# Joining every other pair of weight chunks on VectorE alone, two-byte stores for the rest, and idle matrix products around the first normalization

## The chip, the cores and the metric

The kernel runs on one core of one Trainium2 chip. The metric is the device time of one execution in microseconds, the median of the runs. The names used below: PE is TensorE (matrix products), PEld its weight loads, DVE is VectorE, ACT is ScalarE, POOL is GpSimd and SP the engine that issues most transfers.

## The reference, cut to what matters

Three layers follow each other on 8 batches of 576 tokens and 512 channels: an attention without a score matrix, a Fourier mixing with a normalization and a two-layer network, and a gated network at the end. The weights `w_ch1` and `w_ch2` come in float64 (`np.random.randn(...) * (1/np.sqrt(...))` stays 64 bits wide), which matters for the change.

```
kv  = einsum(softmax_over_tokens(k), v);  a = einsum(softmax_over_channels(q), kv)
u   = a + real(fft(fft(a, axis=1), axis=2))
un  = (u - mean(u)) / sqrt(var(u) + 1e-6)
x   = u + max(un @ w_ch1, 0) @ w_ch2
out = sigmoid(xr @ w_r) * ((max(xk @ w_k, 0) ** 2) @ w_v)      # xk, xr mix x with the token before
```

## The kernel before

The tokens of all batches, 4608, are cut into nine blocks of 512. The main loop takes block after block: for each of 16 column chunks `f` of `w_ch1`, `mm1(f)` makes `un @ w_ch1` (L1093), and two chunks later `mm2` multiplies the result by `w_ch2` (L1116). The last layer follows the same way (L1154, L1207, L1219). Once this loop runs, PE has always something to do, and the work of the next batches (attention, transform, norm) is done beside it.

Before the loop can run, four things must be ready, and they are made beside each other in a stretch that I call the front:

- `attention(0)` (L331 to L431) makes the first batch's `u` from q, k and v.
- `transform(0)` (L464 to L552) does the Fourier mixing as products with constant matrices: `eo`, `eh` and `el` are sums and their split into a rounded and a remaining part, `yh` and `yl` the result of the first products (L509), `pc` and `sd` those of the second (L529), and L545 to L552 add them to `u`.
- `norm(0)`, in two halves of 256 tokens: L616 makes the mean over channels as a product with a matrix of ones, L618 subtracts it into `d`, L620 and L621 square into `sq`, L632 makes the variance, again as a product with ones, L640 to L646 turn it into a reciprocal root `rs`, L658 scales `d`, and L671 and L672 split the result into `unh` and `unl`.
- `front_z` makes 32-bit floats from the 64-bit words of the two weight matrices, in 16 pairs of chunks (`pairs`, 128 x 1024 words each, numbered 0 to 15 here). A pair takes a low shift on DVE (L168), a store on ACT (L169), which writes the top three bits of the low word as one byte into the high word, a high join on DVE (L171), and a sum of squares on ACT (L231). After all pairs of a matrix a scale is known (`scales`, L240 to L250), and `split` (L257 on ACT, L258 on DVE) makes two 16-bit parts of each chunk. The first `mm1` needs the first four chunks split.

A scheduler fixes the order of the instructions of each engine when the program is built; on the chip each engine works through its own list in order and waits where an operand is not ready. So an edit in the front changes the order of all engines.

`warm` makes products whose result nobody reads, with the matrix of ones as the left operand; it writes into one of the two banks `h`. Before the change it stands at two places of the first batch's transform.

Of the kernel before, what the change touches and what calls it, by code (L numbers as in the profile page):

```python
# [10 lines left out]
F16 = mybir.dt.float16  # L11
BF16 = mybir.dt.bfloat16
U32 = mybir.dt.uint32
U8 = mybir.dt.uint8
AF = mybir.ActivationFunctionType
ALU = mybir.AluOpType
AX = mybir.AxisListType
# [11 lines left out]
POOL_K = ()  # L29
BEHIND_X = {(1, 1): 6}  # L30
RATE = 0.4
AHEAD_W = 6
FIRST = 1.0
HOLD = {(2, 0): "c"}
# [14 lines left out]
def net(ctx, tc, q, k, v, w1, w2, mu_k, mu_r, w_k, w_v, w_r, ce_d, se_d, cs_d, ss_d, alt_d, id_d, out):  # L49
    nc = tc.nc  # L50
# [27 lines left out]
    mm = nc.tensor.matmul  # L78
# [82 lines left out]
        nc.sync.dma_start(out=raw.rearrange("p n w -> p (n w)"), in_=src.bitcast(U32)[128 * t:128 * t + 128, 512 * c:512 * c + 512])  # L161
        return raw

    def assemble(raw, x, part=None):

        hi, lo = raw[..., 1], raw[..., 0]
        if part != 1:
            nc.vector.tensor_scalar(out=x, in0=hi, scalar1=3, scalar2=0x3FFFFFFF, op0=ALU.logical_shift_left, op1=ALU.bitwise_and)  # L168
            nc.scalar.activation(out=raw.bitcast(U8)[..., 4], in_=lo, func=AF.Copy, scale=0.9975 * 2.0 ** -29, bias=-0.49)  # L169
        if part != 0:  # L170
            nc.vector.scalar_tensor_tensor(out=x, in0=hi, scalar=0xC0000007, in1=x, op0=ALU.bitwise_and, op1=ALU.bitwise_or)  # L171

    def decode(raw, x):

# [4 lines left out]
    raws = {}  # L179
# [33 lines left out]
    def words_at(w, c):  # L213
        a, b = place[w, c] + 1, place[w, c + 1] + 1
        return wr[:, a:b + 1:b - a]

    def low_parts(k):

        if k < len(pairs):
            assemble(raws[k], words_at(*pairs[k]), 0)  # L220

    def high_parts(k):
        if 0 <= k < len(pairs):
            assemble(raws.pop(k), words_at(*pairs[k]), 1)
            if k + 4 >= AHEAD_W:
                load_pair(k + 4)

# [207 lines left out]
        done_att[0] = b  # L435
        yield 0

    def warm(x, src):

        pt = bank("h", 2)  # L440
        for _ in range(x):
            mm(out=pt[:, 0:128], lhsT=ones, rhs=src, start=True, stop=True)


    done_att = [-1]
# [2 lines left out]
    def transform(b):  # L448
# [11 lines left out]
        if b in (0, 1, 2):  # L460

            for t in range(4):
                for e, op in ((0, ALU.add), (1, ALU.subtract)):
                    tt(out=eo[:, e, t, 1:289], in0=u[:, t, 1:289], in1=u[:, t, S - 1:HALF - 1:-1], op=op)  # L464
                if t == 0 and b == 0:
                    warm(8, eo[:, 0, 0, 1:129])
                if t == 2:
                    nc.scalar.activation(out=x6[0:1, 0:289], in_=eo[0:1, 0, 2, 0:289], func=AF.Copy)
                    tt(out=x6[32:33, 0:289], in0=eo[0:1, 0, 2, 0:289], in1=x6[0:1, 0:289].bitcast(F32), op=ALU.subtract)
                yield 0  # L470
            nc.scalar.activation(out=eo[0:1, :, 2, 0:289], in_=eo[0:1, :, 3, 0:289], func=AF.Copy)
            nc.vector.memset(eo[0:1, 0, 3, 0:289], 0.0)
            for e, op in ((0, ALU.add), (1, ALU.subtract)):
                for g in range(2):
                    tt(out=eo[:, e, g, 0:289], in0=eo[:, e, g, 0:289], in1=eo[:, e, 3 - g, 0:289], op=op)
                    ma = nc.scalar.activation(out=eh[:, e, g, 0:289], in_=eo[:, e, g, 0:289], func=AF.Copy)
                    if b == 0:
                        warm(1, eo[:, e, g, 1:129])
                for g in range(2):
                    mv = tt(out=el[:, e, g, 0:289], in0=eo[:, e, g, 0:289], in1=eh[:, e, g, 0:289].bitcast(F32), op=ALU.subtract)  # L480
            if b < 2:
                mark((2, "a")[b], mv, ma)
            yield 0
        else:
            tt(out=eo[:, 0, :, 1:289], in0=u[:, :, 1:289], in1=back, op=ALU.add)
            yield 0
            tt(out=eo[:, 1, :, 1:289], in0=u[:, :, 1:289], in1=back, op=ALU.subtract)
            nc.scalar.activation(out=x6[0:1, 0:289], in_=eo[0:1, 0, 2, 0:289], func=AF.Copy)
            tt(out=x6[32:33, 0:289], in0=eo[0:1, 0, 2, 0:289], in1=x6[0:1, 0:289].bitcast(F32), op=ALU.subtract)
            nc.scalar.activation(out=eo[0:1, :, 2, 0:289], in_=eo[0:1, :, 3, 0:289], func=AF.Copy)  # L490
            nc.gpsimd.memset(eo[0:1, 0, 3, 0:289], 0.0)
            yield 0
            for e, op in ((0, ALU.add), (1, ALU.subtract)):
                tt(out=eo[:, e, 0:2, 0:289], in0=eo[:, e, 0:2, 0:289], in1=eo[:, e, 3:1:-1, 0:289], op=op)
            for e in range(2):
                nc.scalar.activation(out=eh[:, e, :, 0:289], in_=eo[:, e, 0:2, 0:289], func=AF.Copy)
                tt(out=el[:, e, :, 0:289], in0=eo[:, e, 0:2, 0:289], in1=eh[:, e, :, 0:289].bitcast(F32), op=ALU.subtract)
            yield 0
# [37 lines left out]
        for g in range(2):  # L536
# [2 lines left out]
            nc.scalar.activation(out=pc, in_=pp, func=AF.Copy)  # L539
            yield 1  # L540
            qq = stage2(slice(NK + 128 * g, NK + 128 * g + 128), ssh, ssl)
            tt(out=sd[:, g, 1, :], in0=pc, in1=qq, op=ALU.subtract)
            tt(out=sd[:, g, 0, :], in0=pc, in1=qq, op=ALU.add)
            yield 1
        tt(out=u[:, 0:2, 0:289], in0=u[:, 0:2, 0:289], in1=sd[:, :, 1, 0:289], op=ALU.add)  # L545
        tt(out=u[:, 0:2, S - 1:288:-1], in0=u[:, 0:2, S - 1:288:-1], in1=sd[:, :, 0, 1:288], op=ALU.add)
        pp = stage2(slice(0, 128), csh, csl)
        nc.scalar.activation(out=sd[0:1, 0], in_=sd[0:1, 1], func=AF.Copy)
        ma = nc.scalar.activation(out=sd[0:1, 1], in_=pp[0:1, None, :].to_broadcast([1, 2, NS]), func=AF.Copy)
# [49 lines left out]
    def norm_part(i, sq, d, rs, c0, n):  # L599
# [16 lines left out]
                    mm(out=pt[:, o - c0:o - c0 + m], lhsT=ones, rhs=U[b][:, t, s:s + m], start=(t == 0), stop=(t == 3))  # L616
        for b, s, m, o in segs:
            mv = tt(out=d[:, :, o:o + m], in0=U[b][:, :, s:s + m], in1=pt[:, None, o - c0:o - c0 + m].to_broadcast([128, 4, m]), op=ALU.subtract)  # L618
        yield 1
        nc.scalar.activation(out=sq[:, 0:2, cs], in_=d[:, 0:2, cs], func=AF.Square)  # L620
        ma = nc.scalar.activation(out=sq[:, 2:4, cs], in_=d[:, 2:4, cs], func=AF.Square)  # L621
        yield 0
        if not onpe:
# [14 lines left out]
        w = sq[:, 1, cs]  # L638
        if i in SUMS_F32:
            nc.scalar.activation(out=r, in_=pt[:, 0:n], func=AF.Ln, bias=wsc[:, 7:8])  # L640
            nc.scalar.activation(out=r, in_=r, func=AF.Exp, scale=-0.5)
            yield 1
            tt(out=v, in0=r, in1=r, op=ALU.mult)
            nc.vector.scalar_tensor_tensor(out=v, in0=pt[:, 0:n], scalar=1e-6, in1=v, op0=ALU.add, op1=ALU.mult)
            nc.vector.tensor_scalar(out=v, in0=v, scalar1=-0.5, scalar2=1.5, op0=ALU.mult, op1=ALU.add)
            tt(out=r, in0=r, in1=v, op=ALU.mult)  # L646
        else:
            nc.vector.tensor_scalar(out=v, in0=pt[:, 0:n], scalar1=1e-6, scalar2=None, op0=ALU.add)
            nc.scalar.activation(out=r, in_=v, func=AF.Ln)
# [6 lines left out]
        yield 0  # L656
        for x in range(2):
            (nc.gpsimd.tensor_tensor if i in POOL_N else tt)(out=d[:, 2 * x:2 * x + 2, cs], in0=d[:, 2 * x:2 * x + 2, cs], in1=r[:, None, :].to_broadcast([128, 2, n]), op=ALU.mult)  # L658
            yield 0
        if i == 0:  # L660
            halves_part(0, c0, n)
# [724 lines left out]
```

## Time and profile before

| what | us |
|---|---|
| median of 3 runs | 1475.55 (1475.35 to 1476.8) |
| the profiled execution, its own time | 1476.24 |
| span of that execution in the trace | 1474.5 |
| PE busy in the span | 1407.6 (95%) |
| DVE busy | 989.5 (67%) |
| ACT busy | 705.6 (48%) |

The span is the part of the execution that the trace covers; the profiled execution is 1.7 us longer than its span and 0.7 us above the median. The rate of TensorE's clock is given as the share of full speed that was granted: 1.00 is 2.4 GHz, 0.50 is 1.2 GHz. A matrix product of 32-bit floats shows as two MATMUL records in the trace and as one in the lists of instructions.

### The profile page before, as it was taken

The page shows a single profiled execution, that of the slowest core. Times are in us where ns is not written, and L with a number is a line of the kernel's source. Part 1 is how long each engine was busy: PE and PEld are TensorE (multiplying, and loading weights), DVE is VectorE, ACT ScalarE, POOL GpSimd, SP SyncE. Part 2 cuts the span into 40 slices and gives each one's busy share as a digit, 9 for nine tenths or more (in the row PEclk, how much of TensorE's full clock was granted, in tenths as well). Part 3 has the DMA queues.
Part 4 walks back from the last instruction along what each step waited for, and adds up shares of the span by engine and source line. Part 5 has one row for each costly group of instructions (what it writes and reads, how often), then busy time and mean ns, then how long its engine had stood idle before and what let it go on. Part 6 is the DMA issues. An engine that isn't in the chain of part 4 may idle for free.

```text
span 1474.5 us, 20917 instructions
## 1 busy us (share of the span) xinstructions
PE 1407.6 (95%) x8453; PEld 879.7 (60%) x8453; DVE 989.5 (67%) x1807; ACT 705.6 (48%) x1241; POOL 26.5 (2%) x41
## 2 busy tenths in 40 slices
PE   4559999998999999999999999999999999999998
PEld 3447888996555556556455444445666666666665
DVE  6778676587584765764532476774999788876643
ACT  6895643453342443432321246563766555564421
POOL 0101000000000000000000000000000000000000
PEclk8579999999999999999999999999999999999999
DMA  9731012121110111010010023301011011100001
GB/s 349 251 136 51 1 52 80 51 85 45 51 51 29 51 51 63 17 51 30 0 58 7 32 80 117 118 22 58 29 58 51 8 58 58 50 9 29 30 15 43
DMA packets 38301, 89.47 MB, mean 61 GB/s; under 512 B 5147, under 2 KB 11580, under 8 KB 38204
## 3 DMA queue, kind: packets, MB, share of 16 engines
q1 hardware_dynamic: 37052, 85.30, 16.6%
q0 software_dynamic: 1152, 2.83, 0.6%
q8 instruction: 66, 1.08, 0.3%
q14 instruction: 31, 0.25, 0.1%
HBM read 69.25 MB, written 18.87 MB: 60 GB/s over the span
## 4 chain that ended last, share of the span: by engine, by line
PE 88%; DVE 5%; ACT 4%; issue 1%; DMA 1%; ACTq 0%; DVEq 0%
PE h L1093 24%; PE acc L1116 24%; PE acc L1219 13%; PE h L1154 11%; PE side L1207 6%; PE side L509 2%; PE side L529 2%; PE side L430 2%; PE side L375 1%; ACT u L169 1%; PE side L410 1%; DVE wr L258 1%; DVE wr L171 1%; ACT words L169 1%; DMA kt<-in_k_dram 1%
## 5 line engine op out<-in xcount | busy, mean ns | idle before, releaser
L1093 PE MATMUL h<-unh,wr 128*128 128x512 f16 (+1 forms) x1408 | 381.8, 342 | 3.8 <-ACT unh L671 2.0
L1116 PE MATMUL acc<-hh,wr 128*128 128x512 f16 (+1 forms) x1408 | 370.4, 341 | 0.0
L1093 PEld LDWEIGHTS <-wr 128*128 128x128 f16 x2112 | 203.0, 98 | 169.1 <-issue 7.5
L1116 PEld LDWEIGHTS <-wr 128*128 128x128 f16 x2112 | 201.7, 98 | 160.8 <-issue 3.7
L1093 PE MATMUL h<-unl,wr 128*128 128x512 f16 (+1 forms) x704 | 240.6, 342 | 0.7 <-DVE unl L672 0.7
L1116 PE MATMUL acc<-hl,wr 128*128 128x512 f16 (+1 forms) x704 | 220.0, 341 | 0.0
L1219 PE MATMUL acc<-ring,last 128*128 128x512 f16 x864 | 201.2, 379 | 0.2 <-DVE last L1250 0.2
L1099 DVE SCALAR_TENSOR_TENSOR hl<-h,hh 128x512 f16<-128x512 f32 x144 | 99.0, 687 | 145.8 <-ACT hh L1098 145.2
L1098 ACT ACTIVATE hh<-h 128x512 f16<-128x512 f32 x144 | 85.8, 596 | 180.5 <-PE h L1093 179.8
L1219 PEld LDWEIGHTS <-last 128*128 128x128 f16 x864 | 84.0, 98 | 86.5 <-DVE last L1250 0.7
L1154 PEld LDWEIGHTS <-wkh 128*128 128x128 f16 x1008 | 98.5, 98 | 34.1
L1248 ACT ACTIVATE last<-last,pw 128x512 f32<-128x512 f32 x72 | 51.6, 717 | 106.9 <-DVE last L1247 106.3
L1207 PE MATMUL side<-ring,x 128*128 128x512 f16 x432 | 101.1, 379 | 0.0
L1154 PE MATMUL h<-x,wkh 128*128 128x256 f16 x560 | 95.7, 273 | 0.0
L1169 DVE TENSOR_TENSOR last<-h,last 128x512 f32<-128x512 f32 x90 | 61.8, 687 | 49.9 <-PE h L1154 49.8
L1154 PE MATMUL h<-x,wkl 128*128 128x256 f16 x280 | 76.3, 273 | 0.0
L1154 PE MATMUL h<-last,wkh 128*128 128x256 f16 x448 | 76.1, 273 | 0.0
L1207 PEld LDWEIGHTS <-x 128*128 128x128 f16 x432 | 42.3, 98 | 42.5
L1250 DVE TENSOR_TENSOR last<-last 128x512 f16<-128x512 f32 x72 | 49.5, 687 | 22.1 <-ACT last L1249 21.7
L1154 PE MATMUL h<-last,wkl 128*128 128x256 f16 x224 | 61.1, 273 | 0.0
L883 ACT ACTIVATE aa<-y,ms 128x512 f32<-128x512 f32 x72 | 48.0, 712 | 17.5 <-DVE x L891 12.2
L887 DVE SCALAR_TENSOR_TENSOR aa<-y,ms,aa 128x512 f32<-128x512 f32 x72 | 52.4, 747 | 1.2
(350 smaller groups left out, 2074.2 us busy)
## 6 DMA issues: line engine op xcount, KB each, us to landing
vt<-in_v_dram SPq DMA_DIRECT2D x16, 650.0 KB, 5.0
kt<-in_k_dram SPq DMA_DIRECT2D x16, 576.0 KB, 3.9
qt<-in_q_dram SPq DMA_DIRECT2D x16, 576.0 KB, 3.9
out_dram<-oo SPq DMA_DIRECT2D x36, 256.0 KB, 2.0
y<-yT SPq DMA_DIRECT2D x8, 1026.0 KB, 5.3
u<-in_w_dram SPq DMA_DIRECT2D x16, 512.0 KB, 4.5
words<-in_w_dram SPq DMA_DIRECT2D x10, 512.0 KB, 9.8
raw<-in_w_k_dram SPq DMA_DIRECT2D x16, 256.0 KB, 3.7
```

Source lines behind the costliest of these rows:

```text
L883: nc.scalar.activation(out=a, in_=y[:, t, 0:n], func=AF.Copy, scale=mu[:, w, 1, t:t + 1])
L887: nc.vector.scalar_tensor_tensor(out=a, in0=y[:, t, 1:n + 1], scalar=mu[:, w, 0, t:t + 1], in1=a, op0=ALU.mult, op1=ALU.add)
L1093: mm(out=pt[:, o:o + m], lhsT=a, rhs=c[:, t, o:o + m], start=(t == z == 0), stop=(t == 3 and z == 2))
L1098: ma = nc.scalar.activation(out=hh[:, 0:n], in_=pt[:, 0:n], func=AF.Relu)
L1099: mv = nc.vector.scalar_tensor_tensor(out=hl[:, 0:n], in0=pt[:, 0:n], scalar=0.0, in1=hh[:, 0:n], op0=ALU.max, op1=ALU.subtract)
L1116: mm(out=acc[x][:, o:o + m], lhsT=a, rhs=c[:, o:o + m], start=(f == z == o == 0), stop=(f == NF - 1 and z == 2), skip_group_check=(i < 2))
L1154: mm(out=pt[:, 256 * x:256 * x + 256], lhsT=c[:, u, 128 * x:128 * x + 128], rhs=d[:, u], start=(fresh and x == u == z == 0), stop=(last an ...
L1169: nc.vector.tensor_tensor(out=out, in0=view(pt), in1=addend, op=ALU.add)
L1207: mm(out=pt, lhsT=a[:, v, u, c, o:o + 128], rhs=w[:, t, :], start=(t == y == 0), stop=(t == 3 and y == 2))
L1219: mm(out=acc[x], lhsT=a[:, 128 * x:128 * x + 128], rhs=c[:, f, :], start=(f == z == 0), stop=(f == 7 and z == 2))
L1248: nc.scalar.activation(out=o, in_=o, func=AF.Square, scale=W["pw"][:, 10 + g:11 + g])
L1250: nc.vector.tensor_tensor(out=l2, in0=o, in1=h2, op=ALU.subtract)
```

## The change

Pairs with an even number are joined on DVE alone: in place of ACT's store stands a second join on DVE (new L172), which shifts the low word right by 29 and ors it into the result; the high join then takes only the two top bits of the high word. For odd pairs ACT still stores, now as a two-byte element into the low half of the high word in place of one byte. The same two-byte store is used for the 40 smaller chunks of the last layer's weights. And `warm` is called at 12 more places of the first batch's transform and norm (for batch or block 0 alone); two of the 12 stand in the transform's loop over two column groups, and norm's eight run in each of its two halves (the last of them twice), so that 56 products come on top of the 12 that were there.

```
-    def assemble(raw, x, part=None):
+    def assemble(raw, x, part=None, own=False):
         hi, lo = raw[..., 1], raw[..., 0]
+        join = nc.vector.scalar_tensor_tensor
         if part != 1:
             nc.vector.tensor_scalar(out=x, in0=hi, scalar1=3, scalar2=0x3FFFFFFF, op0=ALU.logical_shift_left, op1=ALU.bitwise_and)
-            nc.scalar.activation(out=raw.bitcast(U8)[..., 4], in_=lo, func=AF.Copy, scale=0.9975 * 2.0 ** -29, bias=-0.49)
+            if own:
+                join(out=x, in0=lo, scalar=29, in1=x, op0=ALU.logical_shift_right, op1=ALU.bitwise_or)
+            else:
+                nc.scalar.activation(out=raw.bitcast(U16)[..., 2], in_=lo, func=AF.Copy, scale=0.9975 * 2.0 ** -29, bias=-0.49)
         if part != 0:
-            nc.vector.scalar_tensor_tensor(out=x, in0=hi, scalar=0xC0000007, in1=x, op0=ALU.bitwise_and, op1=ALU.bitwise_or)
+            join(out=x, in0=hi, scalar=0xC0000000 if own else 0xC0000007, in1=x, op0=ALU.bitwise_and, op1=ALU.bitwise_or)
...
-            assemble(raws[k], words_at(*pairs[k]), 0)
+            assemble(raws[k], words_at(*pairs[k]), 0, k % 2 == OWN)
...
-            assemble(raws.pop(k), words_at(*pairs[k]), 1)
+            assemble(raws.pop(k), words_at(*pairs[k]), 1, k % 2 == OWN)
...
+    def warm(b, x, src):
+
+        if b == 0:
+            pt = bank("h", 2)
...
+            for _ in range(x):
+                mm(out=pt[:, 0:128], lhsT=ones, rhs=src[:, 0:128], start=True, stop=True)
...
             qq = stage2(slice(NK + 128 * g, NK + 128 * g + 128), ssh, ssl)
+            warm(b, 2, pc)
             tt(out=sd[:, g, 1, :], in0=pc, in1=qq, op=ALU.subtract)
+            warm(b, 1, sd[:, g, 1, :])
...
         tt(out=u[:, 0:2, 0:289], in0=u[:, 0:2, 0:289], in1=sd[:, :, 1, 0:289], op=ALU.add)
+        warm(b, 2, sd[:, 1, 0, :])
         tt(out=u[:, 0:2, S - 1:288:-1], in0=u[:, 0:2, S - 1:288:-1], in1=sd[:, :, 0, 1:288], op=ALU.add)
+        warm(b, 2, u[:, 0, 289:417])
...
             mv = tt(out=d[:, :, o:o + m], in0=U[b][:, :, s:s + m], in1=pt[:, None, o - c0:o - c0 + m].to_broadcast([128, 4, m]), op=ALU.subtract)
+        warm(i, 4, d[:, 0, cs])
         yield 1
         nc.scalar.activation(out=sq[:, 0:2, cs], in_=d[:, 0:2, cs], func=AF.Square)
+        warm(i, 2, sq[:, 0, cs])
...
             nc.scalar.activation(out=r, in_=pt[:, 0:n], func=AF.Ln, bias=wsc[:, 7:8])
+            warm(i, 2, r)
             nc.scalar.activation(out=r, in_=r, func=AF.Exp, scale=-0.5)
+            warm(i, 2, r)
             yield 1
             tt(out=v, in0=r, in1=r, op=ALU.mult)
+            warm(i, 2, v)
             nc.vector.scalar_tensor_tensor(out=v, in0=pt[:, 0:n], scalar=1e-6, in1=v, op0=ALU.add, op1=ALU.mult)
             nc.vector.tensor_scalar(out=v, in0=v, scalar1=-0.5, scalar2=1.5, op0=ALU.mult, op1=ALU.add)
+            warm(i, 2, v)
             tt(out=r, in0=r, in1=v, op=ALU.mult)
+            warm(i, 3, r)
...
             (nc.gpsimd.tensor_tensor if i in POOL_N else tt)(out=d[:, 2 * x:2 * x + 2, cs], in0=d[:, 2 * x:2 * x + 2, cs], in1=r[:, None, :].to_broadcast([128, 2, n]), op=ALU.mult)
+            warm(i, 3, d[:, 2 * x, cs])
```

The edits move line numbers: the low shift is L170 in the changed kernel, the new join L172, the store L174, the high join L176, the mean product L627 (was L616), the subtraction L629 (L618), the variance product L645 (L632) and `warm` L450 (L442). Three places show how the lists of instructions change.

VectorE in the middle of the first batch's attention, around the joins of pairs 3, 4 and 5 (they read `u`, `raw` and `words`, in this order). Before:

```order
L360 TENSOR_TENSOR kt<-kt,acc_243 128x1024
L363 TENSOR_TENSOR kt<-kt,acc_243 64x128 x2
L168 TENSOR_SCALAR wr<-words 128x2x512
L171 SCALAR_TENSOR_TENSOR wr<-raw,wr 128x2x512
L331 TENSOR_TENSOR m<-kt 128x256
L333 TENSOR_TENSOR m<-m,kt 128x256 x2
L336 TENSOR_TENSOR m<-m,kt 64x128 x2
L171 SCALAR_TENSOR_TENSOR wr<-words,wr 128x2x512
L354 TENSOR_REDUCE st<-qt 128x18
```

The same stretch in the changed kernel:

```order
L365 TENSOR_TENSOR kt<-kt,acc_243 128x1024
L368 TENSOR_TENSOR kt<-kt,acc_243 64x128 x2
L176 SCALAR_TENSOR_TENSOR wr<-u,wr 128x2x512
L172 SCALAR_TENSOR_TENSOR wr<-raw,wr 128x2x512
L170 TENSOR_SCALAR wr<-words 128x2x512
L336 TENSOR_TENSOR m<-kt 128x256
L176 SCALAR_TENSOR_TENSOR wr<-raw,wr 128x2x512
L338 TENSOR_TENSOR m<-m,kt 128x256
L359 TENSOR_REDUCE st<-qt 128x18
L176 SCALAR_TENSOR_TENSOR wr<-words,wr 128x2x512
```

Pair 4 (`raw`) has a join more and needs no store of ACT's. Between the low shift of pair 5 (`words`) and its high join now stand a high join of pair 4, two maxima and a maximum over q (L359); before it was the high join of pair 4 and five maxima.

VectorE at the end of the first transform (the last two additions to `u`) and the start of norm. Before:

```order
L552 TENSOR_TENSOR u<-u,sd 128x2x287
L171 SCALAR_TENSOR_TENSOR wr<-words,wr 128x2x512
L343 TENSOR_REDUCE wsc<-side_669 128x2
L168 TENSOR_SCALAR wr<-u 128x2x512
L618 TENSOR_TENSOR d<-u,acc_562 128x4x256
L618 TENSOR_TENSOR d<-u,acc_568 128x4x256
```

In the changed kernel:

```order
L176 SCALAR_TENSOR_TENSOR wr<-u,wr 128x2x512
L562 TENSOR_TENSOR u<-u,sd 128x2x289
L563 TENSOR_TENSOR u<-u,sd 128x2x287
L348 TENSOR_REDUCE wsc<-side_749 128x2
L629 TENSOR_TENSOR d<-u,acc_578 128x4x256
L629 TENSOR_TENSOR d<-u,acc_589 128x4x256
L176 SCALAR_TENSOR_TENSOR wr<-u,wr 128x1024
```

The joins of pairs 13 and 14 now stand ahead of the last additions to `u`; between these and the subtraction (L629), which needs the mean from PE, one short instruction is left.

PE in norm, from the mean products to the variance products. Before:

```order
L616 MATMUL acc_562<-u,onesr 128x256 x2
L616 MATMUL acc_568<-u,onesr 128x256 x2
L347 MATMUL side_669<-m,one 128x256
L632 MATMUL side_581<-sq,onesr 128x256 x4
L632 MATMUL acc_588<-sq,onesr 128x256 x4
L410 MATMUL side_733<-ident,qt 128x128 x4
L414 MATMUL side_752<-ident,qt 128x128
L242 MATMUL side_600<-wsc,one 128x1
```

In the changed kernel:

```order
L627 MATMUL acc_578<-u,onesr 128x256 x2
L627 MATMUL acc_589<-u,onesr 128x256 x2
L352 MATMUL side_749<-m,one 128x256
L450 MATMUL h<-d,onesr 128x128 x4
L645 MATMUL side_613<-sq,onesr 128x256 x2
L450 MATMUL h<-d,onesr 128x128 x4
L450 MATMUL h<-sq,onesr 128x128 x2
L645 MATMUL side_613<-sq,onesr 128x256 x2
L645 MATMUL acc_626<-sq,onesr 128x256 x4
L450 MATMUL h<-sq,onesr 128x128 x2
L415 MATMUL side_813<-ident,qt 128x128 x4
L450 MATMUL h<-rs,onesr 128x128 x2
```

Six idle products now stand between the first and the second half of the variance products of the first 256 tokens. Behind the rows shown come 20 more on `rs` and 12 on `d`, all ahead of the first product of the main loop.

## Rows read from the trace of the kernel before

**Rows 1.** Windows: busy time of each engine, granted clock, DMA share

```profile
0.00:119.10 119.10, 62.00 (x271) 50.81 (x271) 89.35 (x162) 91.75 (x132) 5.77 (x15) 0.74 0.63 233
119.10:1474.50 1355.40, 1345.64 (x8183) 828.88 (x8183) 900.15 (x1645) 613.85 (x1110) 20.69 (x26) 1.00 0.14 46
18.00:45.00 27.00, 9.45 (x34) 6.86 (x33) 18.16 (x28) 26.15 (x40) 4.97 (x8) 0.65 0.96 354
45.00:75.00 30.00, 18.62 (x93) 16.81 (x93) 22.19 (x45) 24.43 (x38) 0.00 (x0) 0.63 0.58 213
75.00:97.00 22.00, 12.90 (x59) 10.44 (x58) 18.00 (x28) 20.51 (x25) 0.00 (x0) 0.79 0.59 227
```

**Rows 2.** Waits of DVE, 0 to 119.1 us: total, times, longest

```profile
DVE wr L171 <- ACT words L169: 8.5, 5, 3.3
DVE wr L171 <- ACT u L169: 5.5, 5, 1.8
...
DVE wr L171 <- ACT raw L169: 2.2, 3, 1.3
...
DVE wr L171 <- ACT seh L137: 2.0, 1, 2.0
```

**Rows 3.** Groups on ACT by form, 0 to 125 us: busy, mean ns

```profile
L169 ACT ACTIVATE u<-u 128x1024 uint8<-128x1024 uint32 x8 | 19.7, 2496 | 0.0
L231 ACT ACTIVATE wr<-wr 128x1024 bf16<-128x1024 f32 x16 | 16.9, 1059 | 2.4 <-DVE wr L171 2.2
...
L403 ACT ACTIVATE qT<-side 128x512 f32<-128x512 f32 x4 | 4.7, 1175 | 0.0
...
L364 ACT ACTIVATE kt<-kt 128x1152 f32<-128x1152 f32 x3 | 3.5, 1152 | 0.7 <-DVE kt L363 0.7
L231 ACT ACTIVATION_READ_ACCUMULATOR wr<-wr 128x1 f32 x16 | 3.0, 189 | 0.0
```

**Rows 4.** Groups on DVE by form, 0 to 119.1 us

```profile
L171 DVE SCALAR_TENSOR_TENSOR wr<-u,wr 128x1024 uint32<-128x1024 uint32 x8 | 9.8, 1223 | 7.5 <-ACT u L169 5.5 <-ACT seh L137 2.0
...
L168 DVE TENSOR_SCALAR wr<-u 128x1024 uint32<-128x1024 uint32 x8 | 5.4, 678 | 0.0
...
L354 DVE TENSOR_REDUCE st<-qt 128x18 f32<-128x1152 f32 x4 | 5.4, 1349 | 0.1
...
L333 DVE TENSOR_TENSOR m<-m,kt 128x256 f32<-128x256 f32 x8 | 3.4, 422 | 0.1
```

**Rows 5.** Timeline: high joins of pairs 1, 5 and 15 with their waits

```profile
26.68 1.23 DVE L171 SCALAR_TENSOR_TENSOR wr<-words,wr 128x1024 uint32<-128x1024 uint32 x1 [0.42 <-ACT words L169]
...
46.72 1.23 DVE L171 SCALAR_TENSOR_TENSOR wr<-words,wr 128x1024 uint32<-128x1024 uint32 x1 [3.31 <-ACT words L169]
...
105.63 1.23 DVE L171 SCALAR_TENSOR_TENSOR wr<-u,wr 128x1024 uint32<-128x1024 uint32 x1 [0.41 <-ACT u L169]
```

**Rows 6.** Timeline of DVE: ahead of the subtraction, and the fourth split

```profile
91.04 1.23 DVE L171 SCALAR_TENSOR_TENSOR wr<-words,wr 128x1024 uint32<-128x1024 uint32 x1 [1.65 <-ACT words L169]
92.18 0.42 DVE L343 TENSOR_REDUCE wsc<-side 128x2 f32<-128x256 f32 x1
...
118.31 0.73 DVE L258 SCALAR_TENSOR_TENSOR wr<-wr,wsc 128x512 f16<-128x512 f32 x1
```

**Rows 7.** Timeline of PE: idle products, mean and variance products

```profile
51.82 3.78 PE L442 MATMUL h<-eo,onesr 128*128 128x128 f32 x16 [2.74 <-DVE eo L464]
...
70.64 0.38 PE L442 MATMUL h<-eo,onesr 128*128 128x128 f32 x2
...
89.39 2.68 PE L616 MATMUL acc<-u,onesr 128*128 128x256 f32 x8
...
96.88 3.78 PE L632 MATMUL side<-sq,onesr 128*128 128x256 f32 x8 [1.85 <-ACT sq L620]
100.45 2.28 PE L632 MATMUL acc<-sq,onesr 128*128 128x256 f32 x8
```

**Rows 8.** Window of 5 us at the start of the variance products

```profile
95.00:100.00 5.00, 3.15 (x8) 2.52 (x8) 4.57 (x8) 4.43 (x6) 0.00 (x0) 0.50 0.02 3
```

More of the change, by code (lines that the diff above doesn't have):

```diff
@@ L13 @@
 U32 = mybir.dt.uint32
-U8 = mybir.dt.uint8
+U16 = mybir.dt.uint16
 AF = mybir.ActivationFunctionType
@@ L31 @@
 RATE = 0.4
+OWN = 0
 AHEAD_W = 6
@@ L436, in attention @@
         yield 0
[L438 to L442, printed above, removed]
+    def warm(b, x, src):
+        if b == 0:
+            pt = bank("h", 2)
+            if len(src.shape) > 2:
+                src = src.rearrange(("p a b -> p (a b)", "p a b c -> p (a b c)")[len(src.shape) - 3])
+            for _ in range(x):
+                mm(out=pt[:, 0:128], lhsT=ones, rhs=src[:, 0:128], start=True, stop=True)
     done_att = [-1]
@@ L465, in transform @@
                 if t == 0 and b == 0:
-                    warm(8, eo[:, 0, 0, 1:129])
+                    warm(0, 8, eo[:, 0, 0, 1:129])
                 if t == 2:
@@ L476, in transform @@
                     ma = nc.scalar.activation(out=eh[:, e, g, 0:289], in_=eo[:, e, g, 0:289], func=AF.Copy)
-                    if b == 0:
-                        warm(1, eo[:, e, g, 1:129])
+                    warm(b, 1, eo[:, e, g, 1:129])
                 for g in range(2):
```

## The prediction, made blind

> **What bounds the kernel now.** I read the windows first, cut where PE stops waiting. From 119.1 us on PE is busy 1345.6 of 1355.4 us at full clock; ahead of it 62.0 of 119.1 at a granted 0.74 [rows 1]. So from 119.1 on the time is PE's work and nothing else, which the change leaves as it is: it adds no product there, and the 40 smaller stores of the last layer lie on ACT, which is busy 614 of those 1355 us. The change can win or lose only in the front, by moving the moment when the first four weight chunks are split and the first batch is normalized. The last of these is the fourth split on DVE (L258), which ends at 119.04 [rows 6]; a microsecond there is a microsecond of the total.
>
> What holds the front? In the three windows from 18 to 97 us, 79 us together, ACT is busy 26.15 + 24.43 + 20.51 = 71.1 (90%) and DVE 18.16 + 22.19 + 18.00 = 58.4 (74%) [rows 1]. ACT is the fuller one, and DVE's list of waits says what it does with the rest: the high join L171 waited 8.5 + 5.5 + 2.2 us for ACT's store. The fourth row, 2.0 us "for L137", is the same wait (pair 3; a store had ended just then), so 18.2 us in all [rows 2]. The groups show why: one store takes 2.50 us for 1024 elements, though ACT writes 1024 contiguous two-byte values in 1.06 [rows 3].
>
> **The change, part by part.** I count at DVE, since it does the fourth split: the end of the front is the sum of what DVE does until then and of what it waits. In before that is 89.35 busy and 29.75 idle [rows 1]. The lists of instructions have the same work on DVE ahead of the fourth split in both kernels, but for the eight new joins.
>
> *The new joins.* Each is of the kind and size of the high join, 1.223 us [rows 4]; eight cost 9.8 us of DVE. Nothing hides them: DVE works through its list in order. From 18 to 97 us DVE then has 68.2 us to do and ACT, without eight stores of 2.50, 51.1: the fuller engine changes.
>
> *The waits of the even pairs* vanish with the store. Read pair by pair from the timeline, of which [rows 5] shows the first, the longest and the last of the eight odd ones, the odd pairs hold 13.3 of the 18.2 us and the even ones 4.9. So the even pairs alone cost more than they give: 9.8 against 4.9. The gain must come from the odd pairs, whose store no longer queues behind others.
>
> *The waits of the odd pairs.* What remains is ACT's path to the end of the store less what DVE's list puts ahead of the high join. For pair 5, the worst with 3.31 us [rows 5], I walk both lists of the changed kernel from the end of L368. DVE: three joins of 1.22, a shift of 0.68, two maxima of 0.42, the maximum over q of 1.35: 6.5 us [rows 4]. ACT: two sums of squares of 1.06 + 0.19, two copies of 1.18, an exponential of 1.15, the store of 2.50: 8.5 us [rows 3]. That leaves 1.9 us if both start together, and 1.3 if ACT is a store's tail ahead, as its emptier list suggests. By the same walk I estimate that pair 7 keeps 0.8 to 1.2 (four or five short DVE instructions behind its shift) and pair 13 0.4 (a join and two short ones); the other five have a join and more behind their shift, 2.5 us or over, as long as the store. Together 2.5 to 3.5; I take 2.6.
>
> This holds if the two-byte store takes as long as the one-byte store. No row shows one. Its bounds: 2.50, the row with the same step of eight bytes, and 1.06, the row with the same width [rows 3]. A four-byte store with a step of 16 bytes (L403) takes 1.18 for 512, about twice the contiguous rate, so a step can cost as much as the byte does. I take 2.50, the row with everything alike but the width. At 1.06 all 2.6 us go.
>
> The Trainium skill, SBUF — State Buffer, in its section on the DMA port swizzle, says that accesses run at full rate as long as two of them fall into each 16-byte line. By that rule a step of eight bytes is free, for bytes as for two-byte elements, and the one-byte row of 2.50 us speaks against it. If it nevertheless holds for two bytes, ScalarE: Activation LUTs, What ACT_TABLE_LOAD costs, gives an estimate of 1.04 us for the store (0.186 + 0.833 per thousand elements), and the sum would be that of the first rival below.
>
> *A new wait at the subtraction.* Before, DVE spent the time between the last addition to u and L618 on pair 13 and other work: the join at 91.04 even waited 1.65 [rows 6]. Pairs 13 and 14 now stand earlier, and only the 0.42 of L343 is left in between. The mean products behind the addition took 2.68 us [rows 7], so 2.3 us of wait appear at the clock of before, and about 0.9 if the idle products bring the products to full clock (half of 2.68, less 0.42). I take 1.6.
>
> *The idle products.* One product is two records, 3.78 / 8 = 0.47 us at half clock by the eight of the transform, about half at full clock (0.38 for one with its tail, [rows 7]). They can help where PE is waited for at half clock: the variance products start at a granted 0.50 [rows 8] and take 96.88 to 102.7, 5.9 us for 16 records; at full clock two times 1.9, so 2.1 less. They hurt in the same place: PE's list is worked in order, and six of them stand ahead of the second half of the first variance group, 1.4 us at full clock and 2.8 at half. Net +0.7 to -0.7: I count nothing. They also make DVE wait: the idle products read v and r, which the next instructions overwrite, so L644 has to wait for two products (0.5 to 0.95); some of it lies under ACT's exponentials, and I count 0.3. The 12 on d ahead of the main loop (2.9 us at full clock) lie beside DVE's last two splits with what stands between them, a maximum over q of 1.35 and a subtraction over the same elements.
>
> *Transfers.* Each pair's high join starts the load of a later pair, so the loads move with the joins; the low shifts never waited for data [rows 4], though the transfers were at 0.96 from 18 to 45 us [rows 1]. SP's list changes by one swap, two pairs' loads ahead of a v that is needed much later. I count nothing.
>
> **The sum.** 18.2 - 9.8 - 2.6 - 1.6 - 0.3 = 3.9 us less. The profiled execution (1476.24 with a span of 1474.5) would take 1472.3; it lies 0.7 above the median of 1475.55, and from the median it is **1471.7**.
>
> **The rivals.**
>
> *The two-byte store runs at the contiguous rate* (1.06): the 2.6 us go too, 6.5 less, 1469.0. For it speaks that the one-byte store is slower than every other row on ACT; against it the stepped four-byte row.
>
> *The idle products stand in the way.* If PE stays at half clock through norm, the six products cost 2.8 and save nothing: 3.9 - 2.8 = 1.1, 1474.4. The window at 0.50 speaks for it [rows 8]; that PE has then fewer gaps, against it.
>
> *The odd pairs keep their waits* (the slower side). If what sets the odd waits is not ACT's queue but the place of the shifts in DVE's list, the 13.3 us stay, and the front is 9.8 - 4.9 = 4.9 us longer: 1480.5. It decides from about 6.5 us of remaining odd waits on (18.2 - 9.8 - 1.9). ACT's 90% before speaks against it, since a queue so full is where such waits come from.
>
> *The rest is reshuffled.* All lists behind 119.1 change too. PE waits there only 9.8 us in 1355, so I give this no case of its own but 2 us either way in the range.
>
> **How the numbers follow.** The forecast gets 45%, the fast store 25%, the products in the way 18%, the kept waits 12%. About 0.2% (3 us) is what this measurement can tell from no change, so faster means under 1472.6. The forecast's own range is 1469.7 to 1473.5, four fifths of it under that: 0.36, with nearly all of the fast store 0.60. Slower, over 1478.5, is the kept waits and a sliver of the third: 0.13. The rest, 0.27, is the same. The range takes in the fast store with 2 us more (1467.0) and the products in the way with 3 more (1477.5), and leaves out the kept waits.
>
> **What would show it.** In the changed profile: the waits of the high join for the store fall from 18.2 to 2 or 3 us, mostly at pairs 5 and 7; eight joins of 1.22 at L172; a new wait of DVE at L629 for PE; the fourth split (L263) ends about 4 us earlier, near 115; ACT's busy time to there falls by about 20 us. The duration of L174 settles the first rival at once, the granted clock between 90 and 110 us the second. Wrong would be the prediction if the waits at L176 stay above 6 us, or if PE's idle time behind the front grows.

## The result and the profile after

The changed kernel takes **1459.13 us** (median of 4 runs, 1458.84 to 1459.38) where the kernel before took 1476.17 beside it: a ratio of 0.9884 with a 95% interval of 0.9867 to 0.9901, some 17 us less. The forecast was 1471.7 with a range from 1467.0: the direction was right, the gain more than four times as large as the sum. The profiled spans fell from 1474.5 to 1457.6 us.

The windows of the changed kernel, cut as in [rows 1] (us, then busy time of PE, PEld, DVE, ACT and POOL, granted clock, DMA share, GB/s):

```profile
0.00:119.10 119.10, 78.06 (x448) 67.14 (x449) 103.84 (x181) 80.74 (x138) 5.80 (x15) 0.87 0.65 244
119.10:1457.60 1338.50, 1334.09 (x8119) 821.25 (x8117) 892.08 (x1635) 608.71 (x1095) 20.90 (x26) 1.00 0.14 45
18.00:45.00 27.00, 13.18 (x58) 10.78 (x57) 25.80 (x39) 24.21 (x42) 5.00 (x8) 0.77 1.07 406
45.00:75.00 30.00, 21.30 (x103) 18.77 (x103) 27.48 (x51) 22.37 (x40) 0.00 (x0) 0.69 0.74 271
75.00:97.00 22.00, 16.88 (x102) 14.04 (x100) 17.97 (x28) 16.03 (x25) 0.00 (x0) 1.00 0.22 85
```

From 18 to 75 us DVE is now the full engine (53.3 of 57 us), ACT has gaps, and from 75 us on PE is granted its full clock. The waits of DVE up to the end of the fourth split (total, times, longest), which answer to [rows 2]:

```profile
DVE rs L658 <- ACT rs L655: 2.7, 2, 1.4
DVE m L336 <- DMA kt<-in_k_dram: 1.9, 1, 1.9
DVE sq L617 <- ACT rs L653: 1.5, 1, 1.5
DVE wr L176 <- ACT words L174: 1.5, 2, 1.1
...
DVE sd L550 <- PE side L540: 1.1, 1, 1.1
...
DVE wr L176 <- ACT u L174: 0.8, 1, 0.8
DVE rs L660 <- PE h L450: 0.8, 1, 0.8
...
DVE d L629 <- PE acc L627: 0.2, 1, 0.2
```

The high join waits 2.3 us for ACT's store in place of 18.2. But other waits came: 3.5 us in norm at L658 and L660, 1.5 at L617, which had waited 3.2 for PE before (as L606), and 1.1 in the transform at L550, where 0.2 had been. The new join and the store (which answers to [rows 3]), in the groups of DVE and of ACT (busy, mean ns):

```profile
L172 DVE SCALAR_TENSOR_TENSOR wr<-u,wr 128x1024 uint32<-128x1024 uint32 x4 | 4.9, 1213 | 0.0
```

```profile
L174 ACT ACTIVATE words<-words 128x1024 uint16<-128x1024 uint32 x4 | 10.0, 2511 | 2.6 <-DVE wr L170 2.6
L174 ACT ACTIVATE u<-u 128x1024 uint16<-128x1024 uint32 x4 | 10.0, 2492 | 0.3 <-DVE wr L170 0.3
```

The fourth split ends at 111.69 us, 7.35 earlier than in [rows 6]. Of the 16.9 us of span the other 9.55 were won behind it, where the forecast looked for nothing. Two places hold most of them. From the end of the fourth split to 330 us PE waited 1.1 us before and not at all now. And at the border between block 1 and block 2 (blocks counted from 0) stood a stall that the profile of before shows like this, first as PE's waits from 330 to 360 us, then as two windows:

```profile
PE side L430 <- DVE qTl L405: 2.1, 1, 2.1
PE h L1093 <- ACT unh L671: 2.0, 1, 2.0
PE h L1093 <- DVE unl L672: 0.3, 1, 0.3
```

```profile
345.00:350.00 5.00, 1.68 (x5) 0.98 (x5) 5.00 (x11) 2.46 (x5) 0.00 (x0) 0.70 0.76 248
350.00:355.00 5.00, 4.78 (x16) 2.10 (x16) 4.83 (x7) 0.55 (x2) 0.00 (x0) 0.62 0.21 73
```

PE idles 4.4 us, and behind the idle time its clock is down: in windows of one microsecond it is granted 0.50 from 347 to 353, so that the window from 350 on has 0.62 though it is 96% busy. The changed kernel in the same 30 us:

```profile
330.00:360.00 30.00, 29.85 (x185) 19.47 (x183) 17.28 (x33) 10.27 (x24) 0.00 (x0) 1.00 0.13 39
```

Why PE waited for `unh` and `unl` is read from the timeline of the norm of block 2, whose last step the first product of block 2 needs. Before (DVE's subtraction of the mean, ACT's first rounded part, PE's first product):

```profile
321.74 2.35 DVE L618 TENSOR_TENSOR d<-u,side 128x512 f32<-128x512 f32 x2 [0.51 <-PE side L596]
345.44 1.15 ACT L671 ACTIVATE unh<-d 128x512 f16<-128x512 f32 x2 [2.02 <-DVE d L658]
346.12 0.59 PE L1093 MATMUL h<-unh,wr 128*128 128x512 f16 x2 [1.96 <-ACT unh L671]
```

The same three steps after:

```profile
306.72 2.35 DVE L629 TENSOR_TENSOR d<-u,side 128x512 f32<-128x512 f32 x2 [0.51 <-PE side L607]
329.58 1.77 ACT L690 ACTIVATE unh<-d 128x512 f16<-128x512 f32 x3 [0.86 <-DVE d L676]
333.78 0.38 PE L1112 MATMUL h<-unh,wr 128*128 128x512 f16 x1
```

From the subtraction to the rounded part takes 23.7 us before and 22.9 after, so that chain is no faster. What changed is when it starts against the loop. The first result of block 1 is added into `u` at 343.42 before and 335.27 after (timeline of DVE, L1134 and L1153): the chain had 21.7 us of lead before and has 28.6 now. The difference, 6.9 us, is about a column chunk of block 1 (7.3 us, 16 chunks in 116). PE's list says the same: of the 768 first-layer products of blocks 0 and 1, 720 stood ahead of the mean product of block 2's norm before, and 696 now; a chunk has 24.

The other wait at the border, 2.1 us for `qTl`, belongs to a later attention. Here the order on DVE changed: the last piece of `qTl` stood behind the first additions of block 1 to `u` before and stands ahead of them now. Before, then after:

```profile
343.42 0.86 DVE L1134 SCALAR_TENSOR_TENSOR u<-acc,wsc,u 128x64 f32<-128x64 f32 x2
...
348.52 0.27 DVE L405 TENSOR_TENSOR qTl<-side,qT 128x128 fp32r<-128x128 f32 x1
```

```profile
331.07 0.29 DVE L410 TENSOR_TENSOR qTl<-side,qT 128x128 fp32r<-128x128 f32 x1
...
335.27 0.87 DVE L1153 SCALAR_TENSOR_TENSOR u<-acc,wsc,u 128x64 f32<-128x64 f32 x2
```

### The profile page after: what moved, and what is told of

It reads as the page before. It is cut to its first block, busy times and chain, and to the rows that moved or that the text cites. A ratio compares the mean times of both kernels' runs of the same rounds, so it can differ in the third digit from the quotient of the medians.

```text
span 1457.6 us, 21156 instructions
## 1 busy us (share of the span) xinstructions
PE 1412.1 (97%) x8565; PEld 888.4 (61%) x8565; DVE 995.9 (68%) x1815; ACT 689.5 (47%) x1233; POOL 26.7 (2%) x41
## 4 chain that ended last, share of the span: by engine, by line
PE 92%; DVE 5%; ACT 2%; issue 1%; DMA 0%; ACTq 0%; DVEq 0%
PE h L1112 25%; PE acc L1135 25%; PE acc L1238 13%; PE h L1173 11%; PE side L1226 6%; PE side L536 2%; PE side L516 2%; PE side L435 2%; PE side L380 2%; PE side L415 1%; PE h L450 1%; ACT wr L236 1%; DVE wr L176 0%; ACT words L174 0%; PE side L381 0%
## 5 line engine op out<-in xcount | busy, mean ns | idle before, releaser
L1269 DVE TENSOR_TENSOR last<-last 128x512 f16<-128x512 f32 x72 | 49.4, 686 | 22.1 <-ACT last L1268 21.7
L408 ACT ACTIVATE qT<-side 128x512 fp32r<-128x512 f32 (+3 forms) x44 | 37.0, 841 | 34.5 <-PE side L415 25.1
```

Of the source, the lines that this page charges most:

```text
L408: nc.scalar.activation(out=dst(qT), in_=src, func=AF.Copy)
L1269: nc.vector.tensor_tensor(out=l2, in0=o, in1=h2, op=ALU.subtract)
```

## The experiments

In the forecast the joins were worth 4.2 us and the idle products cost 0.3. To part them I ran each alone, then the idle products of the transform and of norm apart. The texts on record say "second block's mean products" for those of block 2, and "two chunks" where 24 products are one.

**Joins alone.** The change without its new `warm` calls, and with the one-byte store of before.

```
-                nc.scalar.activation(out=raw.bitcast(U16)[..., 2], in_=lo, func=AF.Copy, ...)
+                nc.scalar.activation(out=raw.bitcast(U8)[..., 4], in_=lo, func=AF.Copy, ...)
...
-            warm(b, 2, pc)
...
-        warm(i, 4, d[:, 0, cs])
...
```

> The kernel before with the eight new joins on VectorE alone: one-byte stores for the odd pairs, no new idle products. Theory A (two separate gains: the joins shorten the front by the 4 us of the forecast's sum; the idle products of norm move the second block's mean products two column chunks forward in PE's list, and that takes away the stall of PE at the border between block 1 and block 2): PE's list behind the front is as before, so the stall near 345 us stays, with a granted clock under 0.8 in the 10 us there; time 1471 to 1474. Theory B (the joins do it all: a front that is over earlier lets everything behind it come in time): stall gone, time 1458 to 1462. In both: waits of DVE for ACT's stores 2 to 4 us instead of 18.

Measured: 1463.07 us, ratio 0.9910 (0.9897 to 0.9924). Both theories missed. The stall stays, as A said, but the fourth split ends at 107.29, 11.75 earlier than before and 4.4 earlier than in the changed kernel. So the joins are worth nearly three times the forecast, and the idle products cost time in the front. Its DVE up to the fourth split, window and waits:

```profile
0.00:107.29 107.29, 59.44 (x270) 48.43 (x270) 96.92 (x170) 73.99 (x124) 5.51 (x15) 0.79 0.70 265
```

```profile
DVE m L336 <- DMA kt<-in_k_dram: 2.0, 1, 2.0
DVE wr L176 <- ACT words L174: 2.0, 3, 0.9
DVE d L625 <- PE acc L623: 1.6, 2, 1.2
...
DVE wr L176 <- ACT u L174: 0.8, 1, 0.8
```

**Idle products alone.** The kernel before with the twelve `warm` calls; no pair joined on DVE, one-byte stores (`OWN = 2`, which no pair's number gives).

> The kernel before with the 56 idle products alone: every pair still takes ACT's one-byte store, no new join. Theory A: the stall of PE at the border between block 1 and block 2 is gone (its list has the second block's mean products two chunks earlier), about 9 us, and the variance products run at full clock, which shortens the front by 2 to 4 us: 1462 to 1466, granted clock 1.00 from 75 us on. DVE's waits for ACT's stores stay near 18 us. Theory B (the joins do it all): 1474 to 1477.

Measured: 1472.27 us, ratio 0.9971 (0.9961 to 0.9981). The stall is gone, but the fourth split ends at 123.57, 4.5 later than before. The time lies in neither range, and A's gain in the front is wrong in sign.

**Joins, with the idle products of the transform alone, and of norm alone.** Two kernels: the change without its eight `warm(i, ...)` calls in norm, and without its four new `warm(b, ...)` calls in the transform.

> The changed kernel without the idle products of norm: joins, two-byte stores and the idle products of the transform. Theory A: PE's list behind the front is as before the change, so the stall at the border of blocks 1 and 2 stays; front shorter by the joins' 4 us and perhaps 1 us of clock in the transform: 1469 to 1473. Theory B (joins, or a shorter front by any means, take the stall away): 1458 to 1463. Theory C (the clock alone decides: a warm transform is enough): mean products at full clock and 1460 to 1465.

Measured: 1463.16 us, ratio 0.9911 (0.9897 to 0.9924); stall there, fourth split at 106.16. The time lies in C's range and the mean products run at full clock, as C said, yet C is false: the joins alone take the same time. A has the stall right and the joins too small; the transform's idle products bring 1.1 us in the front.

> The changed kernel without the idle products of the transform: joins, two-byte stores and the idle products of norm. Theory A: the stall at the border is gone as in the changed kernel, the front 0 to 2 us longer than there by the clock of the first products of norm: 1459 to 1462. Theory C (the clock has to be up from the transform on): 1465 to 1472.

Measured: 1459.65 us, ratio 0.9889 (0.9875 to 0.9902); no stall, fourth split at 113.08. As A said. So it is norm's idle products that both remove the stall and lengthen the front. Whether they remove it by keeping PE busy, or only by moving rows in PE's list, the next three tell apart: they have a few idle products each, at places chosen by where the list then has the mean product of block 2.

**One place, early list.** The change with one of its new calls left, `warm(i, 4, d[:, 0, cs])`; 691 to 696 products stand ahead.

> The changed kernel with one of its twelve new places of idle products: the four on d behind norm's subtraction, 8 products in all. The lists show that the second block's mean products then stand 24 to 29 products earlier in PE's list than before, as with all twelve places. Theory A (the place in the list takes the stall away; the other idle products only lengthen the front, by the 4 to 5 us that the fourth split is later than with the joins alone): fourth split at 107 to 109 us, no stall at 345 us, 1453 to 1457. Theory B (the stall is gone because PE is kept busy and at full clock through norm): stall stays, 1461 to 1464.

Measured: 1456.37 us, ratio 0.9864 (0.9850 to 0.9877); fourth split at 107.67, no stall. As A said.

**One place, late list.** The same with only `warm(i, 2, sq[:, 0, cs])` left; 720 stand ahead.

> The control to the one before: again one place of idle products, the two on sq between norm's squares, 4 in all; here PE's list has the second block's mean products where the kernel before has them. Theory A: fourth split at 107 to 109 us, stall of PE at 330 to 360 us of 4 to 5 us and the clock below 1.00 there, 1461 to 1464. Theory B (any idle product in norm helps): 1455 to 1459.

Measured: 1464.40 us, ratio 0.9918 (0.9904 to 0.9931); fourth split at 108.61, PE busy 25.4 of the 30 us from 330 on, at a granted 0.94. The stall stays, as A said; the time is 0.4 us above its range.

**One place and no joins, early list.** The kernel before with only `warm(i, 2, v)` behind norm's first multiplication; 696.

> The kernel before with one place of idle products, the two on v behind norm's first multiplication, 4 in all; no new joins, one-byte stores for all pairs. PE's list has the second block's mean products 24 products earlier. Theory A: the front as before within 1 us (fourth split 118 to 120), no stall at 345 us, 1467 to 1470. Theory B (stall needs the many idle products or the joins): 1475 to 1477.

Measured: 1467.86 us, ratio 0.9944 (0.9932 to 0.9957); fourth split at 120.19, 0.2 behind A's range, no stall. In the rest as A said: four idle products bring 8.9 us where the 56 of the change alone brought 4.1.

**All pairs joined on DVE.** `k % 2 == OWN` becomes `k % 1 == OWN`, no new idle products.

> All 16 pairs joined on VectorE alone, no store on ACT for them, no new idle products. Theory A (the front is DVE's sum of work and waits): against the joins for eight pairs alone (fourth split 107.3, 1463.1) the last 2.8 us of waits for stores go and eight joins of about 1.15 come, so fourth split at 113 to 114 us and 1468 to 1471. Theory D (ACT's load is what holds the front, DVE has room): fourth split at 107 or earlier, 1460 to 1463.

Measured: 1470.38 us, ratio 0.9957 (0.9943 to 0.9970); fourth split at 113.29, no wait of the join. As A said: with eight joins DVE is the full engine, and eight more come on top.

**Adjacent stores.** The change with the odd pairs' store written without a step.

```
-                nc.scalar.activation(out=raw.bitcast(U16)[..., 2], in_=lo, ...)
+                nc.scalar.activation(out=raw.rearrange("p c n w -> p (c n w)").bitcast(U16)[:, 0:lo.shape[1] * lo.shape[2]]...., in_=lo, ...)
```

> The changed kernel with the odd pairs' stores of the two feed-forward matrices written as 1024 adjacent two-byte elements instead of one in every eight bytes; the three bits then don't reach their place, so the weights that it computes with are others. It measures the step of the store and what the remaining waits are worth. Theory S (the step of eight bytes makes the store slow, whatever the width): the store takes 1.0 to 1.3 us instead of 2.51, the high join's 2.3 us of waits go, the fourth split is 1 to 2.5 us earlier (109 to 111) and the time 1456.5 to 1458.5. Theory W (the four-byte integer operand or the conversion makes it slow): 2.4 us or more still, time 1458.5 to 1459.7.

Measured: 1455.03 us, ratio 0.9858 (0.9845 to 0.9872); fourth split at 107.28. The store's groups on ACT, up to 75 us:

```profile
L174 ACT ACTIVATE words<-words 128x1024 uint16<-128x1024 uint32 x4 | 4.6, 1159 | 3.4 <-DVE wr L170 3.4
...
L174 ACT ACTIVATE u<-u 128x1024 uint16<-128x1024 uint32 x3 | 3.4, 1138 | 1.0 <-DVE wr L170 1.0
```

Theory S holds for the store: the step costs 1.35 us, the width nothing. (The run also moves the writes out of the words that ACT reads beside them; L403 of [rows 3] takes 1.18 us for 512 stepped elements where it reads another tile, so the step is slow there too.) The front gained 4.4 us instead of 1 to 2.5, and the time is 1.5 us below S's range: with the 2.3 us of the join's waits the wait at L550 (1.1) went, and L617 fell from 1.5 to 0.7.

**No idle products, early list.** The joins and two-byte stores of the change, none of its new `warm` calls, and `RATE = 0.45` in place of 0.4; 691 to 696.

> The joins and two-byte stores of the changed kernel, none of its twelve places of idle products, and another rate at which weight steps are put in between the steps of the first batch (0.45 instead of 0.40 a step). In PE's list the second block's mean products stand where they do with the one place on d, 24 to 29 products earlier. Theory A (the place in the list alone decides on the stall): 785 to 786.5 us from the end of block 0 to the end of block 8, no stall; in all 1453 to 1459, since the rate moves the front too. Theory B (it takes idle products): 792.5 to 794 us from block 0's end to block 8's, stall at the border, 1461 to 1465.

Measured: **1453.66 us**, ratio 0.9851 (0.9837 to 0.9864), the fastest of all; fourth split at 105.23, PE busy 28.8 of the 30 us from 330 on at full clock, 787.4 us from block 0's end to block 8's. As A said: the stall is gone without one new idle product. The way from block end to block end is 0.9 us above A's bound; PE has a new wait of 1.2 us there, for ACT's `u`.

**Three places, early list.** The change with the two calls in the transform's loop and the one on d.

> The changed kernel with three of its twelve places of idle products: the two in the transform's loop over column groups and the one on d behind norm's subtraction. The list has the early place. Theory A: early list, 785 to 786.5 us from block 0's end to block 8's, and a front like that of the joins with the transform's idle products (fourth split 106 to 107.5), 1455 to 1457. Theory E (each place of idle products lengthens the front): fourth split at 108.5 or later, 1457 to 1459.

Measured: 1456.35 us, ratio 0.9868 (0.9854 to 0.9881); fourth split at 106.83, 785.9 us between the two block ends. As A said.

**The kernel before at another rate.** `RATE = 0.5`, nothing else; 696.

> The kernel before with nothing of the change, and the rate of weight steps at 0.50 instead of 0.40. Its list has the second block's mean products 24 products earlier. Theory A: 785 to 786.5 us from block 0's end to block 8's where the kernel before takes 793.5; the time is 7 to 8 us less than before, plus or minus what the rate does to the front (up to 3): 1465 to 1472. Theory B (it takes joins or idle products): 792.5 to 794 us between the same two points.

Measured: 1473.53 us, ratio 0.9983 (0.9974 to 0.9992). No stall, and 787.0 us between the block ends, 0.5 above A's bound and far from B's; but block 0 ends 3.2 us later than before although the fourth split ends at 114.90, 4.1 earlier. The time misses A's by 1.5 us. From the fourth split to block 0's end PE has 4.5 us idle instead of 1.1 and is busy 4.0 us longer, with 940 records in place of 911; which work came there was not followed.

Side by side (block 0's end: the first addition of its results into `u`, from DVE's timeline; "ahead": first-layer products in PE's list ahead of the mean product of block 2's norm):

| kernel | ahead | fourth split ends | block 0 ends | block 0's to block 8's end | us |
|---|---|---|---|---|---|
| before | 720 | 119.04 | 226.99 | 793.5 | 1476.17 |
| joins alone | 720 | 107.29 | 215.16 | 792.8 | 1463.07 |
| joins, transform's idle products | 720 | 106.16 | 214.35 | 793.1 | 1463.16 |
| joins, one place, late list | 720 | 108.61 | 216.16 | 792.9 | 1464.40 |
| all pairs joined | 720 | 113.29 | 222.94 | 793.3 | 1470.38 |
| idle products alone | 696 | 123.57 | 231.19 | 785.9 | 1472.27 |
| one place, no joins | 696 | 120.19 | 226.40 | 785.7 | 1467.86 |
| before, other rate | 696 | 114.90 | 230.20 | 787.0 | 1473.53 |
| joins, norm's idle products | 696 | 113.08 | 219.90 | 785.3 | 1459.65 |
| **the change** | 696 | 111.69 | 217.94 | 785.7 | 1459.13 |
| adjacent stores | 696 | 107.28 | 213.47 | 785.8 | 1455.03 |
| joins, three places, early list | 691 | 106.83 | 214.33 | 785.9 | 1456.35 |
| joins, one place, early list | 691 | 107.67 | 215.20 | 785.9 | 1456.37 |
| joins, other rate | 691 | 105.23 | 212.55 | 787.4 | 1453.66 |

The fifth column has two values and nothing between, whatever the front does: 793 with the late list, 785 to 787 with the early one. The timelines of all fourteen kernels agree on the reason. In the five with the late list the subtraction of block 2's norm starts 21.5 to 21.7 us ahead of block 1's end and the chain to the rounded part takes 23.6 to 23.8, and PE waits for `unh`, `unl` and `qTl` at the border. In the nine with the early list the lead is 27.9 to 29.6 and the chain takes 21.6 to 24.0, and none of these waits is there. How full DVE is at the border doesn't decide it: from 330 to 360 us it is busy 19.9 us in the joins alone, with the stall, and 27.9 in the idle products alone, without. No run moved that one place by itself, though; the lists of each kernel differ in other rows too.

## Why the prediction was wrong, step by step

**"From 119.1 on the time is PE's work and nothing else"** is the step that failed in kind. The 9.8 us in which PE was not busy there, and the clock below 1.00 behind them, were spread over 1355 us by the window that I read, and I gave "the rest is reshuffled" 2 us either way without looking where they lay. 4.4 of them lay in one place: 2.3 behind a chain of 23.7 us that had 21.7 us of lead, 2.1 behind a piece of `qTl` that stood late in DVE's list. A place in the lists, not time on an engine, decided over 7 to 8 us, and the change moved it. That it did was luck: nothing in the change aims at it, and three of the kernels with joins for half of the pairs keep the stall. The lists were there to be read: 720 and 696 stand in them.

**The sum for the joins** (18.2 - 9.8 - 2.6 - 1.6 = 4.2, by the terms that concern them) was mis-sized: alone they shorten the front by 11.75. By the windows, DVE's idle time up to the fourth split falls from 29.7 to 10.4, 19.3 less, and its busy time rises by 7.6. The terms named fit: the store's waits fall to 2.8 (2.6 forecast), and the mean product is waited for 1.6 (1.6 forecast). In the changed kernel that last wait is 0.2. Two terms were missing. DVE's other waits of the front, 5.5 us (3.2 of L606 for the variance product, 1.3 of L343 and three small ones), I took as staying, and they went. L606's went because the variance products came sooner. Before, a store held ACT until 96.40, with the squares of norm behind it, and the products then began at half clock [rows 8], so that they ended at 102.73, 7.3 us behind the subtraction:

```profile
93.94 2.46 ACT L169 ACTIVATE u<-u 128x1024 uint8<-128x1024 uint32 x1
...
96.15 0.67 ACT L620 ACTIVATE sq<-d 128x512 f32<-128x512 f32 x1
```

With the joins alone they end 2.8 us behind it, at full clock, with PE busy 9.4 of the 10 us from 80 on. The smaller waits were not followed. And the busy time rises by 7.6, not by the joins' 9.8: where nothing is waited for, an instruction starts before the record of the last one ends (a join of 1.22 us is followed after 1.13). The records of DVE add up to 9.7 us more, and 2.2 us more of them overlap.

**The idle products at "+0.7 to -0.7"** were wrong in size. In the front the transform's bring 1.1 to 1.4 us (107.29 to 106.16 without norm's, 113.08 to 111.69 with them), norm's cost 5.5 to 5.8 (106.16 to 111.69, 107.29 to 113.08), and all twelve 4.4. What they were to bring came: the mean products of the changed kernel run at full clock (1.99 us for 8 records) where the joins alone have this, as PE's timeline of that kernel shows:

```profile
84.01 3.78 PE L623 MATMUL acc<-u,onesr 128*128 128x256 f32 x8 [0.60 <-DVE u L558]
...
88.27 1.89 PE L639 MATMUL side<-sq,onesr 128*128 128x256 f32 x8
89.99 1.89 PE L639 MATMUL acc<-sq,onesr 128*128 128x256 f32 x8
```

But the variance products of the joins alone are at full clock already, so nothing was left to win there, and the idle products stand in between. The changed kernel, PE, then ACT and DVE behind it:

```profile
84.42 1.99 PE L627 MATMUL acc<-u,onesr 128*128 128x256 f32 x8 [1.65 <-DVE u L562]
...
88.70 1.03 PE L645 MATMUL side<-sq,onesr 128*128 128x256 f32 x4
89.57 1.05 PE L450 MATMUL h<-d,onesr 128*128 128x128 f32 x8
90.46 0.61 PE L450 MATMUL h<-sq,onesr 128*128 128x128 f32 x4
90.91 1.03 PE L645 MATMUL side<-sq,onesr 128*128 128x256 f32 x4
91.77 1.89 PE L645 MATMUL acc<-sq,onesr 128*128 128x256 f32 x8
...
97.64 1.16 PE L450 MATMUL h<-rs,onesr 128*128 128x128 f32 x8 [0.56 <-ACT rs L655]
```

```profile
97.17 0.42 ACT L655 ACTIVATE rs<-rs 128x256 f32<-128x256 f32 x1 [0.82 <-PE h L450]
```

```profile
97.62 0.43 DVE L658 TENSOR_TENSOR rs<-rs 128x256 f32<-128x256 f32 x1 [1.30 <-ACT rs L655]
98.84 0.42 DVE L660 SCALAR_TENSOR_TENSOR rs<-side,rs 128x256 f32<-128x256 f32 x1 [0.79 <-PE h L450]
```

The second half's variance starts at 91.77 instead of 89.99; then ACT's exponential, which overwrites `rs`, waits for idle products that read it, DVE waits for ACT, and waits again for the next idle products. The forecast had counted DVE's wait (0.3; measured 0.8), not ACT's, nor that both lie in one chain. The waits of DVE at L617, L658 and L660 come to 5.0 us, nearly all of what norm's idle products cost; in the kernel without them (joins and the transform's idle products) none of the three is there. So the second rival's mechanism was real, but at full clock, and at 5.5 us where the forecast had 1.4 at that clock and 2.8 at half; what hid it is the stall that the same products removed.

**The two-byte store at 2.50** was right (2.51 and 2.49), and the first rival false. The rule of the Trainium skill, SBUF — State Buffer, Door 1, by which two accesses to a 16-byte line run at full rate, is not borne out: with such a step the store takes 2.5 us, without it 1.15. By the Trainium skill, ScalarE: Activation LUTs, What ACT_TABLE_LOAD costs, the estimate was 1.04 us, 0.11 under the adjacent store. **"The odd pairs keep their waits"** was false (2.3 us are left of 13.3). **Transfers at nothing** showed no term: the one wait of DVE for a transfer in the front, 2.0 us before, is 1.9.

Put together from the spans: 11.75 from the joins, less 4.4 for the idle products in the front, makes the 7.35 there. Behind it, by the ends of the blocks, block 0 is 1.7 us shorter (1.1 of it PE's waits), block 1 0.9 longer, block 2 6.8 shorter (104.15 us instead of 110.96: 4.4 of idle time, the rest mostly at half clock), and blocks 3 to 8 together 1.9 shorter: 9.5 of the 9.55. What moved blocks 1 and 3 to 8 was not followed.

## What to carry to other kernels

Where an engine is "always busy", still list its waits with their times, and for each chain that feeds it compare its length with its lead; a lead shorter than the chain is a step that any edit of the order can take or give. Compare the place of such a chain's first instruction in the lists of before and after, not only the work. And an idle product that reads a buffer which the next instruction overwrites is a link in that chain: put few of them, on data that nobody waits to overwrite.

## What the runs showed of the hardware

ACT's store of 1024 elements takes 2.5 us with a step of eight bytes, for one-byte and for two-byte elements alike, and 1.15 us for adjacent two-byte ones; what it reads has the same step in all three. After the waits at the border, 4.4 us in all, PE was granted 0.50 from 347 to 353 us, and the window from 350 to 355 has 0.62 at 96% busy: the stall cost more than its idle time, since block 2 took 6.8 us longer than in the changed kernel. With the joins alone, 4.5 us of idle time made block 2 5.5 us longer. And on DVE the price of an instruction among others is the distance of the starts, 1.13 us for a join whose record is 1.22 long.
